# Sparse attention and a mixture of experts on one core: other lists for the experts computed early, whole-row gathers, other waits for indirect transfers

## The chip, the cores and the metric

The kernel runs on one core of a Trainium2 chip. The metric is the device time of one execution in microseconds (us). A core has a matrix engine (TensorE, PE), VectorE (DVE), ScalarE (ACT), GpSimd (POOL) and SyncE (SP); each works through its own instructions in order. In this kernel SP issues all plain transfers and POOL all indirect ones (rows gathered or scattered by a list of indices in SBUF). 16 DMA engines move the data.

## The reference

Attention with 8 batches, 8 heads, 576 positions and head size 64. Heads 0 to 3 are local (a query sees itself and the 31 positions before it), heads 4 to 7 strided (it sees earlier positions equal to its own modulo 32). The result is `x`, 4608 tokens by 512, and goes through eight experts, two for each token:

```
scores = where(mask, q @ k.T / sqrt(64), -1e9)
x      = softmax(scores) @ v                    # [4608, 512]
noisy  = x @ w_gate + log1p(exp(x @ w_noise)) * noise
top2   = the two largest of 8;  top2_w = softmax over these two
out[t] = sum over its two experts: top2_w * (relu(x[t] @ w1[e]) @ w2[e])
```

`w1[e]` is 512 x 1024 and `w2[e]` 1024 x 512, all in float32.

## The kernel before, in words

**Order.** The program is written as `Piece` objects (engine, planned duration, a function that emits instructions, a rank, dependencies). `issue_all` plays them through a planner: for each engine it takes, of the pieces that could start within 120 ns of the first, the one with the lowest rank, and emits it. So the order on every engine is fixed beforehand by planned times. The planner has a model of the DMA engines: `wire` is the time at which they are done, each transfer adds its bytes times `wires` over 270 bytes per ns, and SP's transfers aren't planned far ahead of it. `t0` is a piece's earliest time; `far` is added after a transfer that a piece depends on. A transfer marked `bulk` waits until the model is nearly idle. A piece that writes a PSUM tile and is followed by one that writes a ring buffer starts no earlier than that buffer's first writer: so the first matmul of `layer2` is planned no earlier than the transfer in `previous` that fetches the old output rows, and that one needs the zero fills of those rows.

**Attention.** 32 units (batch, pair of heads, strided or local), in turn. `loads` fetches k, q and v two units ahead, `prep` transposes k and q, `products` makes the scores of both heads, `item` the softmax and the values, `finish` stores the result to `x_dram` and transposes it into `xT`. In `x_dram` a token's 512 numbers lie as four rows of 128, 576 rows apart.

**Routing.** After the four units of a batch, `route` computes its gates and top 2, gives each (token, expert) a place in the expert's list, and writes 12 groups of 96 entries (token, weight, row) to the table `tab` by indirect transfers from POOL (L817). 

**Experts.** A list of at most 1216 places is cut into jobs of two or three blocks of 128 tokens; the last has a half block. `SUBS` names the jobs as (first place, blocks, tail, batches): a job with fewer than 8 batches takes only places that the first batches are known to fill (`AHEAD` keeps later entries behind them), and can be computed while attention is still running. There are 32 jobs and 80 whole blocks. For a job, `gather` reads the entries, makes row indices (`gxx` for x, `gix` for the output) and fetches x by four indirect transfers for each block, each 128 partitions by 512 B (L946): 32 tokens a transfer, so that DVE's transpose of 32x32 squares in `transposes` (L970) turns it into the layout that matmuls need. x is then split into a high and a low part (ACT L974, DVE L976), and so are the weights (`weights_of`, L887 and L888). `layer1` (L1002) multiplies with 96 matmuls a job, `layer2` (L1064) with 24 a block; the output rows are fetched (`previous`, L1042), added to, and scattered back (L1094). Output rows start as zeros, which SP writes in twelve fills of 384 rows (L1148).

In the planner, matmuls of the experts and of attention share PE: for each us of attention one us of expert work may go first (`PACE` 1.0).

**Pacing on POOL.** So that POOL's indirect transfers don't run ahead of the plan, each is given a wait in `issue_all` for the step of ACT or DVE that ends last at least 200 ns before it, by the plan.

Of the kernel before, what the change touches and what calls it, by code (L numbers as in the profile page):

```python
# [22 lines left out]
def kernel(  # L23
# [35 lines left out]
    AHEAD = {2: [(0, 256)], 4: [(0, 512), (1, 256)], 5: [(1, 640)], 7: [(2, 896)]}  # L59
# [99 lines left out]
    v_s = [keep.tile([GP, 2, NJ, D + 1], F32, name=f"v_s{i}") for i in range(2)]  # L159
# [25 lines left out]
    nc.gpsimd.iota(xrow, pattern=[[4 * S, B], [TB, T]], base=0, channel_multiplier=1)  # L185
    qoff = consts.tile([128, 1], F32, name="qoff")
    for i in range(4):
        nc.vector.memset(qoff[32 * i:32 * i + 32, :], float(i * S))
# [102 lines left out]
    def issue_all(expert_banks, t_start):  # L291
# [43 lines left out]
        while ready:  # L335
# [79 lines left out]
    for name, shape, dtype, depth in (  # L415
            ("raw", [LP, 2, LJ, D], F32, 2), ("ord", [LP, LJ, 2, D], F32, 1),
            ("ks", [GP, 2, NJ, D], F32, 1), ("qs", [GP, 2, NJ, D], F32, 1),
            ("mx", [128, 5], F32, 3), ("ex", [128, 5, KW], F32, 2), ("aT", [128, 5, 128], F32, 2),
            ("rs", [128, 6], F32, 2),
            ("xT", [128, S], F32, 6),  # L420
# [14 lines left out]
    def loads(u, rank):  # L435
# [21 lines left out]
        if local:  # L457
# [4 lines left out]
                             [[D, QB], [QB * D, 2 * NBL], [1, D]], 589824)], True)  # L462
# [5 lines left out]
        else:  # L468
            put("v", R["v_s"].new(),
                [(lambda t, h=h: t[:rows, h, :, :D], v, base + h * S * D, [[NJ * D, rows], [D, NJ], [1, D]], 2048 * rows)  # L470
                 for h in range(2)], True)
# [176 lines left out]
    def finish(u, xo, rank):  # L648
# [3 lines left out]
        base = (b * 4 + d) * S * 128  # L652
# [4 lines left out]
        if local:  # L657
            store(lambda t: t[:, :4, :, :].rearrange("r g h d -> r g (h d)"), 0,
                  [[128, 128], [128 * 128, 4], [1, 128]], 262144)
            store(lambda t: t[:QB, 4, :, :].rearrange("r h d -> r (h d)"), 512 * 128, [[128, QB], [1, 128]], 32768)  # L660
        else:
            for half in range(2):

# [583 lines left out]
```

## Time and profile before

| what | us |
|---|---|
| three runs | 1113.36, 1115.05, 1119.16 (median 1115.05) |
| the profiled execution | 1116.99 |
| its span, first to last instruction | 1115.2 |
| PE busy (matmul) | 1066.9 |
| DVE busy | 615.2 |
| ACT busy | 429.9 |
| POOL busy | 606.9 |
| mean granted TensorE clock | 0.970 |

Busy time is the time in which an engine has an instruction at work; matmuls are pipelined, so that of PE says little of how well it is used. Rows of instructions in order of time have the start, the duration, engine, line, operation, output and inputs, a count, and in brackets the idle time before and what ended it. Rows of groups have the line, engine and operation, the shapes, the count, total busy us and mean ns of one, and after a second bar the idle time before them.

### The profile page before, as it was taken

How to read it: one execution, taken by the hardware profiler on the slowest of the kernel's cores; microseconds unless marked ns; L12 is line 12 of the kernel's file. 1: busy time of each engine (PE TensorE's matmuls, PEld its weight loads, DVE VectorE, ACT ScalarE, POOL GpSimd, SP SyncE). 2: the span in 40 equal slices, each digit the busy share in tenths (PEclk: the TensorE clock that was granted, in tenths of full speed). 3: DMA queues.
4: the chain of work that ended last, by engine and by line, in shares of the span. 5: the costliest groups of instructions: out<-in, count | busy, mean ns of one | idle time of the engine just before them, and what ended most of it. 6: DMA issues, size and time to landing. Idle time of an engine off the chain costs nothing.

```text
span 1115.2 us, 23354 instructions
## 1 busy us (share of the span) xinstructions
PE 1066.9 (96%) x8581; PEld 940.5 (84%) x8581; DVE 615.2 (55%) x1618; ACT 429.9 (39%) x1103; POOL 606.9 (54%) x789
## 2 busy tenths in 40 slices
PE   7988889899998999999999999999999999999993
PEld 5767669788887989898998989898988898898992
DVE  4787976867764434655673455345534643473430
ACT  5687966856633211423341223123311321151220
POOL 1044464566656765656666555655646474656510
PEclk6898979999999999999999999999999999999997
DMA  9698997879775532445553226324522452253210
GB/s 189 165 204 199 229 219 172 184 199 248 198 203 102 161 88 72 135 145 148 176 165 117 83 78 195 95 61 115 174 74 68 126 164 69 77 161 92 73 42 22
DMA packets 184886, 153.03 MB, mean 137 GB/s; under 512 B 74695, under 2 KB 155079, under 8 KB 184752
## 3 DMA queue, kind: packets, MB, share of 16 engines
q1 hardware_dynamic: 159664, 92.40, 34.3%
q0 software_dynamic: 25088, 58.87, 17.7%
q8 instruction: 81, 1.33, 0.5%
q14 instruction: 53, 0.43, 0.1%
HBM read 112.86 MB, written 39.39 MB: 137 GB/s over the span
## 4 chain that ended last, share of the span: by engine, by line
PE 66%; DMA 0%; DVE 0%; issue 0%; POOL 0%; POOLq 0%; DVEq 0%
PE bankE L1064 5%; PE bankF L1064 5%; PE bankH L1064 4%; PE bankD L1064 4%; PE bankB L1064 4%; PE bankB L1002 4%; PE bankD L1002 4%; PE bankF L1002 4%; PE bankC L1002 4%; PE bankH L1002 4%; PE bankE L1002 4%; PE bankA L1002 4%; PE bankG L1002 4%; PE bankC L1064 4%; PE bankA L1064 4%; PE bankG L1064 3%
## 5 line engine op out<-in xcount | busy, mean ns | idle before, releaser
L946 POOL DMA_INDIRECT xg<-x_dram,gxx x304 | 307.4, 1011 | 145.0 <-issue 69.9
L1094 POOL DMA_INDIRECT out_dram<-prev,tabt x80 | 83.3, 1041 | 105.0 <-DVE prev L1089 38.5
L817 POOL DMA_INDIRECT tab<-ent,addr x96 | 93.4, 973 | 62.5 <-issue 10.3
L1042 POOL DMA_INDIRECT prev<-out_dram,gix x80 | 78.3, 979 | 80.5 <-DMA out_dram<-prev,tabt 29.4
L970 DVE STREAM_TRANSPOSE xr<-xg 128x512 f32<-128x512 f32 (+1 forms) x80 | 84.3, 1054 | 20.2 <-DMA xg<-x_dram,gxx 18.5
L974 ACT CAST xhi<-xr 128x512 fp32r<-128x512 f32 (+1 forms) x80 | 47.7, 596 | 95.7 <-DVE xr L970 92.7
L976 DVE TENSOR_TENSOR xlo<-xr,xhi 128x512 fp32r<-128x512 f32 (+1 forms) x80 | 53.2, 665 | 26.4 <-ACT xhi L974 25.0
L888 DVE TENSOR_TENSOR w1lo<-wraw,w1hi 128x512 fp32r<-128x512 f32 x80 | 55.0, 690 | 6.6 <-ACT w1hi L887 4.3
L887 ACT CAST w2hi<-wraw 128x512 fp32r<-128x512 f32 x80 | 46.7, 617 | 29.4 <-DMA wraw<-in_moe_w_dram 8.4
L888 DVE TENSOR_TENSOR w2lo<-wraw,w2hi 128x512 fp32r<-128x512 f32 x80 | 52.1, 682 | 3.9 <-ACT w2hi L887 3.3
L887 ACT CAST w1hi<-wraw 128x512 fp32r<-128x512 f32 x80 | 48.6, 614 | 2.5 <-DMA wraw<-in_moe_w_dram 2.4
L1002 PE MATMUL bankB<-xhi,w1hi 128*128 128x256 f32 (+3 forms) x128 | 39.4, 308 | 2.6 <-ACT xhi L974 2.6
L1002 PE MATMUL bankG<-xhi,w1hi 128*128 128x256 f32 (+3 forms) x136 | 41.1, 302 | 0.0
L1002 PE MATMUL bankG<-xhi,w1lo 128*128 128x256 f32 (+3 forms) x136 | 40.7, 300 | 0.0
L1002 PE MATMUL bankG<-xlo,w1hi 128*128 128x256 f32 (+3 forms) x136 | 40.5, 298 | 0.0
L1002 PE MATMUL bankE<-xhi,w1hi 128*128 128x256 f32 (+3 forms) x132 | 39.9, 302 | 0.0
L1002 PE MATMUL bankD<-xhi,w1hi 128*128 128x256 f32 (+3 forms) x132 | 39.8, 302 | 0.0
L1002 PE MATMUL bankC<-xhi,w1hi 128*128 128x256 f32 (+3 forms) x132 | 39.7, 301 | 0.0
L1002 PE MATMUL bankB<-xlo,w1hi 128*128 128x256 f32 (+3 forms) x128 | 38.8, 303 | 0.7 <-DVE xlo L976 0.7
L1002 PE MATMUL bankD<-xhi,w1lo 128*128 128x256 f32 (+3 forms) x132 | 39.4, 298 | 0.0
L1002 PE MATMUL bankC<-xhi,w1lo 128*128 128x256 f32 (+3 forms) x132 | 39.4, 298 | 0.0
L1002 PE MATMUL bankE<-xhi,w1lo 128*128 128x256 f32 (+3 forms) x132 | 39.4, 298 | 0.0
(614 smaller groups left out, 3474.3 us busy)
## 6 DMA issues: line engine op xcount, KB each, us to landing
wraw<-in_moe_w_dram SPq DMA_DIRECT2D x160, 256.0 KB
out_dram<-zeros SPq DMA_DIRECT2D x12, 768.0 KB
xg<-x_dram,gxx POOLq DMA_INDIRECT x304
ks<-in_k_dram SPq DMA_DIRECT2D x15, 320.0 KB
qs<-in_q_dram SPq DMA_DIRECT2D x15, 320.0 KB
v_s<-in_v_dram SPq DMA_DIRECT2D x30, 160.0 KB
raw<-in_k_dram SPq DMA_DIRECT2D x16, 288.0 KB
v_l<-in_v_dram SPq DMA_DIRECT2D x16, 288.0 KB
```

The lines of the kernel that those rows point to most:

```text
L817: st = nc.gpsimd.indirect_dma_start(out=tab, out_offset=bass.IndirectOffsetOnAxis(ap=s["addr"].t[:, t, kk:kk + 1], axis=0), in_=s["ent"].t ...
L887: Piece("ACT", act(512) + 30, lambda o: nc.scalar.copy(hi.t, raw.t), rank, read=[raw], alloc=[hi], expert=True)
L888: Piece("DVE", dve(512), lambda o: nc.vector.tensor_tensor(lo.t, raw.t, hi.t.bitcast(F32), ALU.subtract), rank, read=[raw, hi], alloc=[lo] ...
L946: dma(lambda o, i=i, g=g, xg=xg: nc.gpsimd.indirect_dma_start(out=xg.t[:, g, :], out_offset=None, in_=x_dram[:4 * known, :], in_offset=bas ...
L970: Piece("DVE", dve(4 * rows), lambda o, xg=xg, xr=xr, ng=ng, rows=rows: nc.vector.transpose(xr.t[:, :, :rows].rearrange("p c (g i) -> p g ...
L974: Piece("ACT", act(4 * rows), lambda o, xr=xr, rows=rows, cols=cols: nc.scalar.copy(xh.t[:, :, cols], xr.t[:, :, :rows]), rank, read=[xr], ...
L976: Piece("DVE", dve(4 * rows), lambda o, xr=xr, rows=rows, cols=cols: nc.vector.tensor_tensor(xl.t[:, :, cols], xr.t[:, :, :rows], xh.t[:, ...
L1002: nc.tensor.matmul(ps.t[:, :width], a.t[:, 128 * d:128 * d + 128], c.t[:, d, :width], start=(m == 0), stop=(m == len(todo) - 1))
L1042: dma(lambda o: nc.gpsimd.indirect_dma_start(out=pv.t[:rows, :], out_offset=None, in_=out[:known, :], in_offset=bass.IndirectOffsetOnAxis( ...
L1064: nc.tensor.matmul(ps.t, HT[n, f][p[0]].t[:, cols], W2[n][f][p[1]].t, start=(m == 0), stop=(m == len(todo) - 1))
L1094: st = nc.gpsimd.indirect_dma_start(out=out[:known, :], out_offset=bass.IndirectOffsetOnAxis(ap=tb.t[:rows, i, 0:1], axis=0), in_=pv.t[:ro ...
```

## The change

- **Early lists.** Jobs known early follow the lists of two, three, five and seven batches: 14 blocks in six jobs, where there were 16 blocks in seven (two, four, five and seven batches). Their `gather` has a rank by batch (`turn`), as their entry and weight loads had before.
- **Whole rows.** `x_dram` now holds a token's 512 numbers in one piece. Early jobs fetch a block with one transfer, 2 KB for each of 128 partitions, by the output's indices; they read no `tabx` and make no `gxx`. Their transposes are four matmuls on PE into a PSUM bank, reading every fourth number. Jobs over all batches gather as before, with other row numbers.
- **Stores.** Strided units store x in pieces of 512 B instead of 1 KB.
- **Strided values** are loaded in lines of 2 KB into a buffer `vraw` and copied to their places by ACT or DVE. The `xT` ring has 5 buffers instead of 6.
- **Pacing.** An indirect transfer waits for DVE's last step in its time, and for ACT's only where DVE has none.
- **Planner's figures.** v's local load counts its real bytes (half of before), narrow rows cost 1.65 instead of 1.45, local k and q 1.2 instead of 1.0, DVE's transposes 8 ns a row instead of about 4, entry loads start 4 us after the scatters; zero fills are due at 26, 36, 46, 56, 66 us and then from 111 us in steps of 10, instead of from 50 in steps of 18.

```diff
-    AHEAD = {2: [(0, 256)], 4: [(0, 512), (1, 256)], 5: [(1, 640)], 7: [(2, 896)]}
+    AHEAD = {2: [(0, 256)], 3: [(1, 384)], 5: [(1, 640), (2, 640)], 7: [(2, 896)]}
-        [(0, 2, 0, 2), (256, 2, 0, 4), (512, 3, 0, B), (896, 2, 64, B)],
-        [(0, 2, 0, 4), (256, 3, 0, 5), (640, 2, 0, B), (896, 2, 64, B)],
-        [(0, 3, 0, 7), (384, 2, 0, 7), (640, 2, 0, 7), (896, 2, 64, B)],
+        [(0, 2, 0, 2), (256, 3, 0, B), (640, 2, 0, B), (896, 2, 64, B)],
+        [(0, 3, 0, 3), (384, 2, 0, 5), (640, 2, 0, B), (896, 2, 64, B)],
+        [(0, 3, 0, 5), (384, 2, 0, 5), (640, 2, 0, 7), (896, 2, 64, B)],
...
-                behind = [x for m in marks.values() for x in m[-40:] if x[0].end + 200 <= t]
-                if behind:
-                    x = max(behind, key=lambda x: x[0].end)
-                    if x[0].end > paced[0]:
+                for engine in ("DVE", "ACT"):
+                    behind = [x for x in marks[engine][-40:] if paced[0] < x[0].end <= t - 200]
+                    if behind:
+                        x = max(behind, key=lambda x: x[0].end)
                         for y in last if isinstance(last, list) else [last]:
                             tc.add_manual_dep(...)
+                        break
...
-                    nbytes, rank, wires={D: 1.45, 4 * D: 1.2}.get(dims[-1][1], 1.0),
+                    nbytes, rank, wires={D: 1.65, LJ * D: 1.2}.get(dims[-1][1], 1.0),
...
+            slot = res["v"] = R["v_s"].new()
+            for h in range(2):
+                put(f"v{h}raw", R["vraw"].new(), [(lambda t: t[:rows].rearrange("p j d -> p (j d)"), v, base + h * S * D,
+                                                   [[NJ * D, rows], [1, NJ * D]], 2048 * rows)], True)
+                def spread(o, h=h, raw=res[f"v{h}raw"]):
+                    copy(o.e, slot.t[:G, h, :, :D], raw.t[:G])
+                Piece("ANY", {"ACT": act(NJ * D), "DVE": 75 + 0.52 * NJ * D}, spread, rank, ...)
...
-        base = (b * 4 + d) * S * 128
+        base = b * S * DM + d * 128
...
+        def turn(n):
+            hb = jobs[n][1][3]
+            return None if hb == B else 20 * NP * (hb - 1) + 10 * NP
         def gather(n, rank):
             e, (start, nb, tail, hb) = jobs[n]
+            rank = rank if hb == B else turn(n)
+            whole = hb < B
...
+            for i in range(nb) if whole else ():
+                xg = R["xg"].new()
+                dma(lambda o, i=i, xg=xg: nc.gpsimd.indirect_dma_start(
+                    out=xg.t.rearrange("p g c -> p (g c)"), out_offset=None,
+                    in_=x_dram.rearrange("(t q) c -> t (q c)", q=4)[:known, :],
+                    in_offset=bass.IndirectOffsetOnAxis(ap=gi.t[:, i:i + 1], axis=0)),
+                    262144, rank, eng="POOL", read=[gi], after=known_stores[hb], expert=True, alloc=[xg])
...
+                if hb < B:
+                    xr = Slot()
+                    def tr(o, xg=xg, xr=xr):
+                        xv = xg.t.rearrange("p g c -> p (g c)").rearrange("p (x c) -> p c x", c=ND)
+                        for c in range(ND):
+                            nc.tensor.transpose(xr.t[:, 128 * c:128 * c + 128], xv[:, c, :], ident)
+                    Piece("PE", 108 * ND, tr, rank, read=[xg], psum=xr, expert=True)
...
-            ER - 1, t0=50000 + 18000 * c, bulk=True))
+            ER - 1, t0=26000 + 10000 * c + 35000 * (c >= 5), bulk=True))
```

More of the change, by code (lines that the diff above doesn't have):

```diff
@@ L158 @@
     v_l = [keep.tile([KW, 2, NBL, D + 1], F32, name=f"v_l{i}") for i in range(2)]
-    v_s = [keep.tile([GP, 2, NJ, D + 1], F32, name=f"v_s{i}") for i in range(2)]
+    v_s = [keep.tile([G, 2, NJ, D + 1], F32, name=f"v_s{i}") for i in range(2)]
     v_0 = [keep.tile([G, 2, D + 1], F32, name=f"v_0{i}") for i in range(2)]
@@ L468, in loads @@
         else:
-            put("v", R["v_s"].new(),
-                [(lambda t, h=h: t[:rows, h, :, :D], v, base + h * S * D, [[NJ * D, rows], [D, NJ], [1, D]], 2048 * rows)
-                 for h in range(2)], True)
+            slot = res["v"] = R["v_s"].new()
[4 more added lines that the diff above has]
+                    copy(o.e, slot.t[:G, h, :, :D], raw.t[:G])
+                Piece("ANY", {"ACT": act(NJ * D), "DVE": 75 + 0.52 * NJ * D}, spread, rank, read=[res[f"v{h}raw"]],
+                      **{"write" if h else "alloc": [slot]})
             put("v0", R["v_0"].new(),
@@ L664, in finish @@
                 store(lambda t, half=half: t[64 * half:64 * half + 64, :4, :, :].rearrange(
-                    "r (m g) h d -> r m (g h d)", m=2),
-                      (QB + 2 * half) * 128, [[NJ * 128, QB], [4 * 128, 2], [1, 256]], 131072)
-            store(lambda t: t[:QB, 4, :, :].rearrange("r h d -> r (h d)"), 0, [[128, QB], [1, 128]], 32768)
+                    "r (m g) h d -> r m g (h d)", m=2),
+                      (QB + 2 * half) * DM, [[NJ * DM, QB], [4 * DM, 2], [DM, 2], [1, 128]], 131072)
+            store(lambda t: t[:QB, 4, :, :].rearrange("r h d -> r (h d)"), 0, [[DM, QB], [1, 128]], 32768)
         xt = R["xT"].new()
@@ L863 @@
             ("tabt", [128, 3, 3], I32, 3), ("gix", [128, 3], I32, 3), ("tabx", [128, 12, 3], I32, 2),
-            ("gxx", [128, 3, 4], I32, 2), ("xg", [128, 4, 128], F32, 2), ("xr", [128, ND, 128], F32, 1),
+            ("gxx", [128, 3, 4], I32, 2), ("xg", [128, 4, 128], F32, 2), ("xr", [128, ND * 128], F32, 1),
             ("xhi", [128, ND, WID], F32R, 1), ("xlo", [128, ND, WID], F32R, 1),
@@ L899, in experts @@
         G_, XH, HT = {}, {}, {}
+        def turn(n):
+            hb = jobs[n][1][3]
+            return None if hb == B else 20 * NP * (hb - 1) + 10 * NP
         def gather(n, rank):
             e, (start, nb, tail, hb) = jobs[n]
+            rank = rank if hb == B else turn(n)
             known = hb * S
-            tb, gi, tx, gx = R["tabt"].new(), R["gix"].new(), R["tabx"].new(), R["gxx"].new()
+            whole = hb < B
+            tb, gi = R["tabt"].new(), R["gix"].new()
+            tx, gx = (None, None) if whole else (R["tabx"].new(), R["gxx"].new())
             def entries(dst, p0, n, how, bytes_, dims):
@@ L916, in load @@
                         early_loads.append((ld, hb))
-                dma(load, bytes_, rank if hb == B else 20 * NP * (hb - 1) + 10 * NP, after=known_tab[hb], expert=True, **how)
-            entries(lambda: tx.t[:, :4 * nb, :].rearrange("p b c -> p (b c)"), start, 128 * nb, {"alloc": [tx]}, 16384,
-                    [[0, 4], [12 * nb, 32], [1, 12 * nb]])
+                dma(load, bytes_, rank if hb == B else 20 * NP * (hb - 1) + 10 * NP, after=known_tab[hb], expert=True,
+                    far=4000, **how)
+            if not whole:
+                entries(lambda: tx.t[:, :4 * nb, :].rearrange("p b c -> p (b c)"), start, 128 * nb, {"alloc": [tx]}, 16384,
+                        [[0, 4], [12 * nb, 32], [1, 12 * nb]])
             ng = tail // 32
@@ L931, in gather @@
                         [[3, tail], [1, 3]])
-            rows_known = 4 * known - 3 * S - 1
+            rows_known = 4 * known - 4
             def xindices(o):
@@ L939, in xindices @@
                                             qoff[:, 0:1], op0=ALU.min, op1=ALU.add)
-            Piece("POOL", 360 if tail else 230, xindices, rank, read=[tx] + ([tx2] if tail else []), alloc=[gx],
-                  expert=True)
+            if not whole:
+                Piece("POOL", 360 if tail else 230, xindices, rank, read=[tx] + ([tx2] if tail else []), alloc=[gx],
+                      expert=True)
             xs = []
-            for i in range(nb + (tail > 0)):
+            for i in () if whole else range(nb + (tail > 0)):
                 xg = R["xg"].new()
@@ L965, in transposes @@
             for i in range(nb + (tail > 0)):
-                xg, xr = G_[n][2][i], R["xr"].new()
+                xg = G_[n][2][i]
                 rows = 128 if i < nb else tail
@@ L1101, in layer2 @@
             out_done[e].append(dma(scatter, rows * 2048, rank, eng="POOL", read=[pv, tb], expert=True))
-        def turn(n):
-            hb = jobs[n][1][3]
-            return None if hb == B else 20 * NP * (hb - 1) + 10 * NP
         W2 = {}
```

35 lines of the change are left out of this document (20 added, 15 removed).

## The prediction

> **What bounds the kernel now.** I read the page's head first, then the busy time by stretch, then PE's waits and the POOL and SP queues in order of time where PE is not full.
>
> ```profile
> span 1115.2 us, 23354 instructions
> ...
> PE 1066.9 (96%) x8581; PEld 940.5 (84%) x8581; DVE 615.2 (55%) x1618; ACT 429.9 (39%) x1103; POOL 606.9 (54%) x789
> ```
>
> The next rows cut the span into stretches. Columns: window, its length, then busy us of PE, PEld, DVE, ACT, POOL, the granted TensorE clock, the DMA share, GB/s.
>
> ```profile
> 0.00:132.00 132.00, 112.81 (x1719) 91.65 (x1719) 96.57 (x411) 98.57 (x297) 36.97 (x98) 0.87 0.90 194
> 132.00:160.00 28.00, 24.43 (x369) 19.72 (x369) 22.61 (x101) 20.77 (x64) 18.35 (x31) 0.84 1.10 234
> 160.00:220.00 60.00, 55.30 (x848) 47.45 (x845) 45.11 (x165) 43.21 (x138) 32.34 (x57) 0.93 0.86 185
> 220.00:340.00 120.00, 119.47 (x1305) 103.88 (x1304) 85.00 (x309) 67.69 (x190) 74.45 (x115) 1.00 0.80 207
> 340.00:380.00 40.00, 36.75 (x177) 32.88 (x176) 18.29 (x28) 11.05 (x22) 26.42 (x34) 0.96 0.52 135
> 380.00:1100.00 720.00, 718.10 (x4176) 644.94 (x4174) 347.61 (x607) 188.61 (x397) 418.26 (x458) 1.00 0.37 110
> 1100.00:1115.00 15.00, 0.00 (x0) 0.00 (x0) 0.00 (x0) 0.00 (x0) 0.15 (x1) 0.61 0.05 20
> ```
>
> From 380 to 1100 PE idles 1.9 us in 720 at full clock. That part is matmul work which the change leaves alone: 80 blocks and 32 jobs before and after, with the same widths. The last 15 us are the final scatter and the end. So the time can change only before 380 us, by PE's idle time, its clock, or its work. There, attention alone does not fill PE; expert blocks computed early do. While they run (220 to 340) PE is full, before that it is not.
>
> Where the early work starts is read from the queues. First POOL:
>
> ```profile
> 112.20 0.91 POOL L817 DMA_INDIRECT tab<-ent,addr  x1 [0.21 <-DVE mx L576]
> ...
> 144.12 1.06 POOL L946 DMA_INDIRECT xg<-x_dram,gxx  x1 [1.23 <-issue]
> ...
> 154.24 0.94 POOL L946 DMA_INDIRECT xg<-x_dram,gxx  x1 [1.10 <-DVE ns L791]
> ```
>
> Then SP's issues, then PE:
>
> ```profile
> 119.07 0.66 SPq L908 DMA_DIRECT2D tabx<-tab  x1
> ```
>
> ```profile
> 175.10 0.63 SPq L1148 DMA_DIRECT2D out_dram<-zeros  x1
> ```
>
> ```profile
> 167.78 0.36 PE L1002 MATMUL bankB<-xhi,w1hi 128*128 128x256 f32 x1
> ```
>
> ```profile
> 220.19 0.48 PE L1064 MATMUL bankD<-w2hi,hhi 128*128 128x512 f32 x1
> ```
>
> The table entries of batches 0 and 1 are written by 113.1 and read at 119, but the first gather starts at 144, behind batch 2's twelve table scatters on POOL, and takes eight transfers to 155. Layer 1 of the first job starts at 168. Its layer 2 starts only at 220, since the planner puts it no earlier than the fetch of the old output rows, which needs three of the zero fills; the second is issued at 175, the third after it.
>
> **The change, part by part.**
>
> *Early jobs first in their turn, one gather a block, zero fills earlier.* A job with a list known early now has its gather ranked by batch, so ahead of batch 2's scatters; it needs no tabx load and no gxx step, and 2 transfers where there were 8. A gather lands like this in the chain that ended last:
>
> ```profile
> 355.67 3.52 DMA xg<-x_dram,gxx
> ```
>
> From the entry load at 119 I estimate 3.5 us to land (taken as for a gather), 2.5 for two transfers of 1.27, 3.5 to land, and 1.9 for transposes and both splits (0.46 and twice 0.69, rows below). That is 130.4 at the earliest; I take 138, for the 4 us that the planner now adds after the scatters and for the queues' order. With fills due from 26 us in steps of 10, layer 2 follows layer 1, and a three-block list of batch 2 comes next instead of a two-block list of batch 3.
>
> What PE then wins, by window, as idle plus clock loss (busy x (1 - clock)):
> - 132 to 160: 3.57 + 24.43 x 0.16 = 7.5; with work from 138 on I count 5.0.
> - 160 to 220: 4.70 + 55.30 x 0.07 = 8.6; I count 8.0, as 220 to 340 shows 0.5 idle in 120 us with early work at hand.
> - 340 to 380: 3.25 + 36.75 x 0.04 = 4.7. This is a gather behind the last scatters:
>
> ```profile
> 347.63 0.91 POOL L817 DMA_INDIRECT tab<-ent,addr  x1 [0.23 <-issue]
> 348.85 0.97 POOL L946 DMA_INDIRECT xg<-x_dram,gxx  x1 [0.30 <-issue]
> ...
> 355.67 1.27 POOL L946 DMA_INDIRECT xg<-x_dram,gxx  x1 [0.85 <-ACT xhi L974]
> ```
>
> The third block of a three-block early job is fetched after batch 7's scatters. The new list for seven batches is two blocks, fetched by two transfers that go ahead of those scatters. I count 4.5.
>
> Together -17.5 us, between 0 and -20.8.
>
> *Transposes of the 14 early blocks move from DVE to PE.* Four 128x128 transposes a block:
>
> ```profile
> 111.66 0.63 PE L681 MATMUL bankH<-ident,xo 128*128 128x128 f32 x4 [1.04 <-DVE xo L630]
> 112.12 0.60 PE L590 MATMUL bankB<-ident,ex 128*72 128x128 f32 x4
> ```
>
> Four such cost 0.46 us of PE's time to the next instruction, so 14 x 0.46 = +6.4 us, all of it on the path, as PE is full by then. Up to 0.63 each, 8.8, without overlap. DVE loses 14 transposes:
>
> ```profile
> L970 DVE STREAM_TRANSPOSE xr<-xg 128x512 f32<-128x512 f32 x72 | 79.3, 1101 | 20.0 <-DMA xg<-x_dram,gxx 18.5 <-issue 0.4
> L976 DVE TENSOR_TENSOR xlo<-xr,xhi 128x512 fp32r<-128x512 f32 x72 | 49.7, 691 | 22.6 <-ACT xhi L974 21.3
> ...
> L283 ACT COPY ord<-raw 96x768 f32<-96x768 f32 x26 | 21.6, 832 | 0.8 <-PE bankC L497 0.3
> ```
>
> 14 x 1.10 = 15.4 us of DVE while PE is the bound: 0.
>
> *Values of the strided heads in long lines, then spread.* Each of 32 loads has 80 packets of 2 KB instead of 640 of 256 B (two of them 72 and 576), and a copy of 72x512 is added. By the 768-wide ACT copy that is at most 0.55 us, 32 in all. Only what lies before the early work counts: in 132 us some 3.3 of 8 batches, 13 copies, 7.2 us of engine time. DVE and ACT are 73 and 75% busy there, and PE waits there for them:
>
> ```profile
> PE bankA L681 <- DVE xo L630: 2.0, 1, 2.0
> PE bankF L609 <- ACT aT L283: 1.4, 1, 1.4
> PE bankA L497 <- ACT ord L283: 1.1, 1, 1.1
> ```
>
> So between 0 and +7.2; as two engines share it and a quarter of them is free, I take +1.5. The packets:
>
> ```profile
> q1 hardware_dynamic: 159664, 92.40, 34.3%
> ```
>
> 34.3% of 16 x 1115.2 us over 159,664 packets is 38 ns a packet. 30 x 560 + 2 x 504 = 17,808 packets fewer are at most 42.6 us of all 16 engines, 17 of it before 132, and nothing if time goes by bytes. The x_dram stores of the strided heads now go in 512 B pieces instead of 1 KB: 32 x 128 packets more, at most 9.8 us by the same price. Five zero fills of 786 KB brought before 132 cost 4.1 us each at 194 GB/s: 20 us at most. DMA is 90% busy there, but what ends PE's waits is DVE and ACT, and loads are issued two units ahead; I take 0 for the net, between -3 and +8, the planner's halved bytes for v_l and its other new prices included, since they only change when SP issues; if that cover is gone a fill holds the loads behind it on SP's queue by its 4.1 us.
>
> *POOL.* 42 transfers fewer:
>
> ```profile
> L946 POOL DMA_INDIRECT xg<-x_dram,gxx x304 | 307.4, 1011 | 145.0 <-issue 69.9 <-DVE xr L970 22.4 <-ACT hhi L1021 17.3
> ```
>
> 42 x 1.01 = 42 us off POOL, which is 54% busy: 0 by itself. Putting each transfer behind a DVE step rather than the latest of DVE and ACT can only choose an earlier or equal step while a DVE step lies in the window, so it costs nothing as long as DVE keeps to its plan; what is queued behind such a wait are the table scatters and gathers, and PE would wait for them. Bounds: all 17.3 us of waits on ACT gone or as many new ones on DVE, off PE's path but for the first gather; 0. The xT ring of 5 instead of 6 still holds a batch's four and one more: 0. SP issues fewer tabx loads; the entry loads' 4 us exist in the plan only.
>
> *Handover to the whole lists.* 14 early blocks instead of 16 have to last until the first gather over all batches. Block cost, layer 1 of a three-block job (8 groups) and layer 2:
>
> ```profile
> 378.46 2.08 PE bankA L1002 x12
> 380.54 5.58 PE bankB L1064 x24
> ```
>
> 8 x 2.08 / 3 + 5.6 = 11.15 us a block, so 156 + 6.4 = 162.5 us. Batch 7's gate is here:
>
> ```profile
> 318.49 1.50 PE L727 MATMUL bankB<-xT,wg 128*32 128x192 f32 x24
> ```
>
> Its scatters end at 348.5, 30 us later; then some 22.2 us by the durations above (entries 3.5, ten transfers at 1.27, landing 3.5, DVE transpose and splits 2.5): 52.2 in all. The expert matmuls of 132 to 318 are two groups:
>
> ```profile
> 132.00:318.00 186.00, 39.99 (x288) 35.54 (x288) 0.95 0.87 205
> ```
>
> ```profile
> 132.00:318.00 186.00, 33.44 (x125) 22.09 (x126) 0.95 0.87 205
> ```
>
> By the stretches above PE works about 177 us in that time, so attention is 104 of it. The kernel gives early work at most an equal share, so 104 are used by the gate and 58.5 are left for 52.2. Before, 178 - 73 = 105 were left. The cover just holds; I take +0.5, between 0 and +18 (if the route is as slow as that or the share is passed).
>
> **Sum.** -17.5 + 6.4 + 1.5 + 0.5 = -9.1. The profiled execution took 1116.99 (its span and 1.8 around it): 1107.9. It stands 1.9 above the median of the three runs, so I predict 1106 for the median. 0.5% is 5.6 us, about what a measurement of this kernel can tell from no change.
>
> **The rivals.**
>
> *The early stage gains too (0.13).* Against me: 19.2 us idle and a clock of 0.87 before 132, with DMA at 90%. If the long lines let loads land sooner, a third of the first stretch's idle goes, about 6 to 9 us more: 1098. What speaks against it: the waits end on DVE and ACT, which get more work.
>
> *Transposes with a 16-byte step cost PE double (0.14).* The new transposes read every fourth word of a row. DVE's transpose reads so too and takes 1101 ns, where its subtraction of as many elements takes 691; no matmul of this trace loads its weights with such a step. Doubled, the four cost 0.92 us: +6.4 more, and 1112.5, no change. A rule speaks for it: the Trainium skill, page "SBUF — State Buffer", section "Door 1: The DMA port swizzle", says that SBUF is read in lines of 16 bytes, and that accesses which go to a new line each time pay for it. It gives no price; the two DVE rows agree in direction.
>
> *The gap is filled late (0.12).* The second early job is now another expert's, so 16 weight tiles must be loaded and split between 140 and 175, where the DMA share is 0.86 or more and DVE and ACT are 72 to 81% busy. If its layer 1 waits until about 200, half of the 13.0 goes: 1112.5, no change.
>
> *Starved at the handover (0.16).* Place: between the end of the 14 blocks and the first gather over eight batches. Price: one us of idle per us of cover missing, the clock falling with it. It decides the sign when 15 us are missing, that is when the route from gate to splits takes 73 us instead of 52.2, or early work passes its share by that much: 1124. For it: two blocks, 22 us, fewer. Against it: attention alone never ran as slowly as that.
>
> **How the numbers follow.** My forecast has 0.45 (1106, by itself 1101 to 1110); 0.13 for 1098, 0.14 and 0.12 for 1112.5, 0.16 for 1124. Faster is 0.45 + 0.13 = 0.58, same 0.26, slower 0.16. The range is 1094 to 1120: the low end is all of the 20.8 and some of the early stage, the high end leaves out most of the last case.
>
> **What would show it.** Right: the first L1002 matmul by 140 and the first L1064 soon after; 132 to 220 with under 2 us idle and the clock at 1.00; 14 groups of four transposes at about 0.46 us; no idle between 340 and 400; 262 rather than 304 gathers. Wrong: groups of four transposes near 0.9 us; PE waiting for xhi after the last early block; a first stretch longer because loads queue behind zero fills.

## The result and the profile after

The changed kernel takes 1108.62 us (median; 1103.93 to 1112.45 over 6 runs), the kernel before 1115.88 us beside it (1113.36 to 1119.16, 6 runs): a ratio of 0.9927, 95% interval 0.9901 to 0.9952. In a later session, beside other kernels, it took 1107.69 against 1116.11, ratio 0.9928 (0.9903 to 0.9953). So it is 0.7% faster, 2.6 us from the predicted 1106. The medians differ by 7.3 us. The two profiled executions, 1116.99 and 1107.29, differ by 9.7, since the one is slower and the other faster than its median. How these 9.7 us came about is another matter.

The head of the page, two of its groups and its main DMA queue:

```profile
span 1105.5 us, 23346 instructions
...
PE 1064.2 (96%) x8637; PEld 939.5 (85%) x8637; DVE 605.6 (55%) x1604; ACT 434.7 (39%) x1135; POOL 563.3 (51%) x741
...
q1 hardware_dynamic: 145160, 92.31, 33.4%
...
L964 POOL DMA_INDIRECT xg<-x_dram,gxx x248 | 255.1, 1029 | 101.8 <-issue 55.2
...
L978 POOL DMA_INDIRECT xg<-x_dram,gix x14 | 14.3, 1024 | 57.1 <-PE bankB L1003 40.4
```

There are 248 + 14 = 262 gathers, as forecast, and one number that was not: of the 57.1 us that POOL idled ahead of whole-row gathers, 40.4 were one kind of wait, on PE.

The stretches, with the columns of those shown of before (PE, PEld, DVE, ACT, POOL, clock, DMA share, GB/s):

```profile
0.00:132.00 132.00, 115.26 (x1780) 93.40 (x1782) 103.01 (x422) 100.44 (x314) 38.68 (x96) 0.90 0.93 210
132.00:160.00 28.00, 27.29 (x388) 23.59 (x385) 23.72 (x102) 24.68 (x73) 13.26 (x24) 1.00 0.89 211
160.00:220.00 60.00, 54.09 (x885) 45.96 (x887) 48.40 (x177) 48.49 (x151) 29.24 (x56) 0.94 0.96 222
220.00:340.00 120.00, 119.48 (x1228) 104.26 (x1221) 70.86 (x271) 61.59 (x178) 39.57 (x68) 1.00 0.61 165
340.00:380.00 40.00, 35.65 (x206) 31.52 (x205) 15.97 (x29) 10.69 (x23) 25.69 (x44) 1.00 0.56 159
380.00:1090.00 710.00, 710.00 (x4166) 639.13 (x4165) 342.87 (x606) 188.85 (x398) 415.86 (x455) 1.00 0.37 112
```

PE's loss in a stretch, reckoned as in the prediction (idle time plus busy time by one minus the clock):

| stretch | before | after | gained | predicted |
|---|---|---|---|---|
| 0 to 132 | 33.9 | 28.3 | 5.6 | -1.5 (the copies) |
| 132 to 160 | 7.5 | 0.7 | 6.8 | 5.0 |
| 160 to 220 | 8.6 | 9.2 | -0.6 | 8.0 |
| 220 to 340 | 0.5 | 0.5 | 0 | 0 |
| 340 to 380 | 4.7 | 4.35 | 0.4 | 4.5 |

That is 12.2 us in all. Busy time by the clock, summed over the stretches, is PE's work: 1042.9 us before and 1049.4 after (with its last 2.4 us, behind 1090, at full clock), 6.5 more, which I read as the new transposes. The 6.5 is not exact: the clock is given with two digits, and 0.005 of it is 0.6 us in the first stretch and 3.6 in the last. And the ends differ: POOL's last scatter in each kernel, before and then after.

```profile
1099.17 0.98 POOL L1094 DMA_INDIRECT out_dram<-prev,tabt  x1 [4.12 <-DVE prev L1089]
```

```profile
1093.50 0.98 POOL L1134 DMA_INDIRECT out_dram<-prev,tabt  x1 [4.09 <-DVE prev L1129]
```

From there to the end of the span it is 16.0 us before (1115.2 - 1099.17) and 12.0 after (1105.5 - 1093.50), with nothing busy but the transfer itself, whose packets are through some 2.5 us after its issue in both. Together 12.2 - 6.5 + 4.0 = 9.7, the whole difference. This sum has to come out, as what a stretch does not lose is counted as work; it checks the arithmetic and not the causes. So two of the three gains that I forecast did not come, and two came that I had not counted (the first stretch and the end).

Where the first two early jobs stand (PE, SP and POOL in order of time):

```profile
146.47 0.38 PE L1042 MATMUL bankB<-xhi,w1hi 128*128 128x256 f32 x1
...
215.96 0.50 PE L1104 MATMUL bankB<-w2hi,hhi 128*128 128x512 f32 x1
```

```profile
69.06 0.60 SPq L1184 DMA_DIRECT2D out_dram<-zeros  x1
...
203.51 1.44 SPq L1184 DMA_DIRECT2D out_dram<-zeros  x1
```

```profile
213.07 0.98 POOL L1082 DMA_INDIRECT prev<-out_dram,gix  x1 [0.55 <-DVE aT L286]
```

Layer 1 starts 21 us sooner (146.5 for 167.8). Layer 2 does not follow: 216.0 for 220.2. Its first matmul is planned behind the fetch of the old rows at 213, that behind the third zero fill, and the third fill is issued at 203.5, though it was due at 46. A fill is a bulk transfer, and those wait until the model of the DMA engines is nearly idle; after the second, at 69, that is not so for 134 us.

The other stretch, on POOL and then on DVE:

```profile
276.61 0.94 POOL L824 DMA_INDIRECT tab<-ent,addr  x1 [0.22 <-POOL spacer L823]
...
317.94 0.98 POOL L978 DMA_INDIRECT xg<-x_dram,gix  x1 [40.39 <-PE bankB L1003]
...
339.46 0.99 POOL L1082 DMA_INDIRECT prev<-out_dram,gix  x1 [3.29 <-issue]
```

```profile
344.63 0.75 DVE L1129 SCALAR_TENSOR_TENSOR prev<-bankA,tabt,prev 128x512 f32<-128x512 f32 x1 [18.44 <-DMA prev<-out_dram,gix]
```

The gather at 317.94 is the third block of a three-block job. There are two `xg` buffers, so it can't start before PE has transposed that job's first block, and POOL stands for 40 us after the first of a batch's twelve table scatters. The rest of these scatters, the fetch of old rows at 339 and DVE's sum at 344.6 come late in turn, and PE idles 4.35 us between 340 and 380.

### The profile page after: what moved, and what is told of

Read it like the earlier page. It is cut to its first block, busy times and chain, and to the rows that moved or that the text cites. A ratio compares the mean times of both kernels' runs of the same rounds, so it can differ in the third digit from the quotient of the medians.

```text
span 1105.5 us, 23346 instructions
## 1 busy us (share of the span) xinstructions
PE 1064.2 (96%) x8637; PEld 939.5 (85%) x8637; DVE 605.6 (55%) x1604; ACT 434.7 (39%) x1135; POOL 563.3 (51%) x741
## 3 DMA queue, kind: packets, MB, share of 16 engines
q1 hardware_dynamic: 145160, 92.31, 33.4%
## 4 chain that ended last, share of the span: by engine, by line
PE 83%; DMA 6%; ACT 4%; DVE 3%; issue 1%; POOL 1%; SPq 0%; POOLq 0%; DVEq 0%; ACTq 0%
PE bankB L1104 6%; PE bankG L1104 5%; PE bankE L1104 5%; PE bankA L1104 5%; PE bankE L1042 5%; PE bankC L1042 5%; PE bankC L1104 5%; PE bankF L1042 5%; PE bankD L1042 5%; PE bankA L1042 4%; PE bankB L1042 4%; PE bankF L1104 4%; PE bankH L1042 4%; PE bankG L1042 4%; PE bankH L1104 4%; PE bankD L1104 3%
## 5 line engine op out<-in xcount | busy, mean ns | idle before, releaser
L964 POOL DMA_INDIRECT xg<-x_dram,gxx x248 | 255.1, 1029 | 101.8 <-issue 55.2
L824 POOL DMA_INDIRECT tab<-ent,addr x96 | 92.7, 965 | 57.1 <-issue 20.4
L1007 DVE STREAM_TRANSPOSE xr<-xg 128x512 f32<-128x512 f32 (+1 forms) x66 | 68.5, 1039 | 23.5 <-DMA xg<-x_dram,gxx 21.1
L1014 ACT CAST xhi<-xr 128x512 fp32r<-128x512 f32 (+1 forms) x66 | 39.0, 591 | 72.9 <-DVE xr L1007 72.9
L1016 DVE TENSOR_TENSOR xlo<-xr,xhi 128x512 fp32r<-128x512 f32 (+1 forms) x66 | 43.5, 659 | 19.2 <-ACT xhi L1014 17.9
L978 POOL DMA_INDIRECT xg<-x_dram,gix x14 | 14.3, 1024 | 57.1 <-PE bankB L1003 40.4
L1042 PE MATMUL bankH<-xhi,w1hi 128*128 128x256 f32 (+3 forms) x128 | 38.6, 302 | 1.4 <-DVE prev L1129 1.4
L1042 PE MATMUL bankA<-xhi,w1hi 128*128 128x256 f32 (+3 forms) x128 | 38.3, 299 | 1.7 <-DVE prev L1129 1.7
L1042 PE MATMUL bankE<-xlo,w1hi 128*128 128x256 f32 (+3 forms) x132 | 39.2, 297 | 0.0
L1042 PE MATMUL bankF<-xhi,w1hi 128*128 128x256 f32 (+3 forms) x128 | 38.3, 300 | 0.0
```

The source lines that it names most:

```text
L824: st = nc.gpsimd.indirect_dma_start(out=tab, out_offset=bass.IndirectOffsetOnAxis(ap=s["addr"].t[:, t, kk:kk + 1], axis=0), in_=s["ent"].t ...
L964: dma(lambda o, i=i, g=g, xg=xg: nc.gpsimd.indirect_dma_start(out=xg.t[:, g, :], out_offset=None, in_=x_dram[:4 * known, :], in_offset=bas ...
L978: dma(lambda o, i=i, xg=xg: nc.gpsimd.indirect_dma_start(out=xg.t.rearrange("p g c -> p (g c)"), out_offset=None, in_=x_dram.rearrange("(t ...
L1007: Piece("DVE", 8 * rows, lambda o, xg=xg, xr=xr, ng=ng, rows=rows: nc.vector.transpose(xr.t.rearrange("p (c x) -> p c x", c=ND)[:, :, :row ...
L1014: Piece("ACT", act(4 * rows), lambda o, view=view, cols=cols: nc.scalar.copy(xh.t[:, :, cols], view()), rank, read=[xr], expert=True, **{h ...
L1016: Piece("DVE", dve(4 * rows), lambda o, view=view, cols=cols: nc.vector.tensor_tensor(xl.t[:, :, cols], view(), xh.t[:, :, cols].bitcast(F ...
```

## The experiments

The kernels ran in three groups of four, each group on one chip and beside the kernel before. On the second of these chips the kernel before took 1116.11 us; on the first and third 1171.88 and 1171.06. Ratios of different chips are not set against each other below.

**First chip (before: 1171.88, 1167.87 to 1181.37).** First, three zero fills ahead of the bulk rule:

```diff
-            ER - 1, t0=26000 + 10000 * c + 35000 * (c >= 5), bulk=True))
+            35 + 20 * c if c < 3 else ER - 1, t0=26000 + 10000 * c + 35000 * (c >= 5), bulk=c >= 3))
```

> The first three zero fills are issued ahead of other transfers (due at 26, 36, 46 us) instead of when the transfer model is idle; all else as in the changed kernel. My theory: the hole that stays in PE from 170 to 216 us (5.9 us idle in 160 to 220 and a clock of 0.94, 9.1 us lost together) is there because layer 2 of the first early job is planned behind the fetch of old output rows, and that behind the third fill, issued at 203. Then layer 2 starts by about 175, 160 to 220 loses under 3 us, and the kernel takes 1099 to 1104. Rival: the hole is the second early job's weights, or the transfers' load, and early fills only push loads back: layer 2 still late or a longer first stretch, 1107 to 1113.

Measured: 1151.08, ratio 0.982 (0.9787 to 0.9853). Layer 2 comes at 180.8, near the 175 of the theory, but 160 to 220 loses 8.5 us and not under 3. Next, the third gather behind the batch's scatters:

```diff
-                    262144, rank, eng="POOL", read=[gi], after=known_stores[hb], expert=True, alloc=[xg])
+                    262144, rank if i < 2 else ER, eng="POOL", read=[gi], after=known_stores[hb], expert=True, alloc=[xg])
```

> The third block of a three-block early job is gathered at the low rank of the expert work, so behind the table scatters of the batch; all else as in the changed kernel. My theory: with two xg buffers the third gather waits on POOL until PE has transposed the first block (40.4 us at 277 to 318), which holds the scatters of batch 6, then a fetch of output rows, on which DVE waits 18.4 us and PE 4.4 us in 340 to 360. Then no POOL wait above 20 us, PE idle in 340 to 380 under 1.5 us, and 1103 to 1107. Rival: that wait is covered and the idle time at 340 comes from the weights that land late (wraw waits of 20 us on ScalarE): no change, 1107 to 1110.

Measured: 1141.58, ratio 0.9755 (0.9718 to 0.9791). Neither sign of the theory came: POOL still waits 23.1 us, and PE idles 4.8 us from 340 to 380. Then the strided values as before:

```diff
-            slot = res["v"] = R["v_s"].new()
-            for h in range(2):
-                put(f"v{h}raw", R["vraw"].new(), ...)
...
+            put("v", R["v_s"].new(),
+                [(lambda t, h=h: t[:rows, h, :, :D], v, base + h * S * D, [[NJ * D, rows], [D, NJ], [1, D]], 2048 * rows)
+                 for h in range(2)], True)
```

> The changed kernel with the strided values loaded in short lines of 256 B straight to their places, as before, without vraw and the spreading copies. My theory: the first 132 us got 5.7 us cheaper (idle 19.2 to 16.7, clock 0.87 to 0.90) because the long lines relieve the DMA engines; undone, the first stretch loses 3 to 6 us again: 1111 to 1115. Rival: that part is the planner's new order, and the copies on ScalarE and VectorE cost what the packets save: 1106 to 1110.

Measured: 1160.86, ratio 0.9893 (0.985 to 0.9936). Its first 132 us lose 34.7, where the others of this chip lose 34.6 to 36.6; the third chip takes this up again. Last, the old pacing:

```diff
-                for engine in ("DVE", "ACT"):
-                    behind = [x for x in marks[engine][-40:] if paced[0] < x[0].end <= t - 200]
...
+                    behind = [x for m in marks.values() for x in m[-40:] if x[0].end + 200 <= t]
```

> The changed kernel with the old rule for POOL's waits: the latest step of ScalarE and VectorE rather than VectorE's. My theory: POOL is off the path except for the first gathers, so nothing within the measurement: 1106 to 1111. Rival: the waits on ScalarE held the scatters and gathers, and this is a good part of the gain: 1112 to 1116.

Measured: 1156.94, ratio 0.9877 (0.9834 to 0.992).

What follows. The changed kernel itself did not run on this chip, so the four can only be set against each other. Among them the late third gather is the fastest, by 9.5 us and more. The stretches 220 to 340 of the early fills and then of the late third gather:

```profile
220.00:340.00 120.00, 106.00 (x1228) 87.64 (x1227) 63.85 (x233) 62.97 (x185) 40.86 (x69) 0.91 0.71 188
```

```profile
220.00:340.00 120.00, 114.31 (x1342) 95.92 (x1339) 72.04 (x263) 68.58 (x206) 44.01 (x80) 1.00 0.71 190
```

With fills alone, layer 2 starts sooner (180.8, where the late gather has 236.5). The early work is used up while POOL stands 33.1 us before a third gather (from 320 to 340 PE runs no layer 1 and idles 8.2 us): the idle time has only moved. The wait is still there, 39.99 us long, with the old pacing, which clears the new pacing of it. With the third gather late, POOL also waits for PE before it, 23.1 us, but after the last table scatter of that batch (at 320.84); the next batch's begin at 367.

**Second chip (before: 1116.11, 1112.7 to 1120.0, 11 runs).** The changed kernel itself:

> The changed kernel itself, unchanged, as the partner of the other runs. Theory (what the first trace of it showed is planned into the kernel, not an accident of that run): layer 1 of the first early job between 140 and 160 us, its layer 2 not before 200 us because the third zero fill is issued after 195 us, and one wait of 30 to 45 us on GpSimd ahead of a third whole-row gather. Ratio to the kernel before 0.980 to 0.993. Rival (the first trace caught one unlucky execution): third fill and third gather without those waits here, and a ratio near 0.980.

Measured: 1107.69 (1104.46 to 1110.94). Third fill at 201.6, layer 1 at 144.2, layer 2 at 214.0, one wait of 40.39 us on POOL. The theory holds: what the first trace showed is in the order of the program.

Both repairs together (the two edits above):

> Two edits together: the first three zero fills get an early rank of their own, and the third gather of a three-block early job gets the experts' rank (behind the batch's table scatters). Theory (two separate waits, both of the plan): the first layer 2 comes by 200 us instead of after 200 to 234, no wait of over 20 us on GpSimd ahead of a third gather; PE's idle time and clock loss from 160 to 380 us fall below that of either edit alone; 0.970 of the kernel before or less, 5 us or more under the late third gather alone. Rival (early work that starts sooner is also used up sooner, and the fills hold loads behind them in the first stretch): the gap moves to between 300 and 420 us, and the time is equal to or up to 8 us above that of the late third gather alone (0.9755).

Measured: 1106.58, ratio 0.9913 (0.9888 to 0.9938). The rival is right about the place (between 300 and 420 us); its time can't be set against the late gather's alone, which ran on another chip. The stretches:

```profile
0.00:132.00 132.00, 113.94 (x1721) 92.52 (x1725) 101.06 (x424) 96.48 (x303) 37.12 (x95) 0.86 0.96 211
...
160.00:220.00 60.00, 59.41 (x731) 52.27 (x730) 45.88 (x154) 44.28 (x125) 30.88 (x52) 1.00 0.90 223
...
340.00:380.00 40.00, 40.00 (x254) 34.22 (x253) 13.53 (x54) 6.83 (x19) 17.40 (x32) 1.00 0.14 42
380.00:420.00 40.00, 30.68 (x176) 27.25 (x175) 10.71 (x20) 5.66 (x13) 18.81 (x22) 0.88 0.22 64
```

```profile
170.28 0.48 PE L1104 MATMUL bankD<-w2hi,hhi 128*128 128x512 f32 x1
```

Layer 2 starts at 170 and both predicted gains appear in full: 160 to 220 loses 0.6 us, 340 to 380 none. They are given back twice. The first stretch loses 34.0 us for the changed kernel's 27.1 beside it, with the three fills issued at 30, 42 and 56; and at the handover the early work has run out, 9.3 us idle and 3.7 us of clock between 380 and 420.

The early gathers at the experts' rank again, which puts a third gather behind the scatters too:

```diff
-            rank = rank if hb == B else turn(n)
```

> One part undone: the early jobs' gathers have the experts' rank again instead of one by their batch; the lists, transposes, whole-row gathers, fills and long lines stay. Theory (the new rank is what brings the first early job forward, and also what puts a third gather ahead of the scatters): the first whole-row gather moves from 130 to 140 us or later and layer 1 of the first job to 158 us or later, 2 to 5 us lost before 220 us; the 30 to 45 us wait on GpSimd is gone, 3 to 5 us won between 300 and 400 us; time within 4 us of the changed kernel. Rival (the rank is the gain and the wait costs nothing, as GpSimd is half idle): 5 us or more slower than the changed kernel.

Measured: 1104.32 (1102.39 to 1105.21), ratio 0.9892 (0.9868 to 0.9915), 3.4 us under the changed kernel.

```profile
132.00:160.00 28.00, 25.89 (x416) 21.43 (x412) 25.80 (x108) 24.55 (x80) 15.51 (x29) 1.00 1.08 240
160.00:220.00 60.00, 55.36 (x850) 47.46 (x852) 47.15 (x170) 47.89 (x144) 27.58 (x50) 0.97 0.90 210
...
340.00:380.00 40.00, 40.00 (x240) 36.38 (x239) 10.42 (x19) 7.36 (x17) 19.84 (x26) 1.00 0.31 91
```

```profile
274.85 0.96 POOL L977 DMA_INDIRECT xg<-x_dram,gix  x1 [2.87 <-PE bankB L1002]
...
317.88 0.98 POOL L977 DMA_INDIRECT xg<-x_dram,gix  x1 [7.80 <-PE bankB L1002]
```

The theory holds, with a smaller cost than it gave: the first gather moves to 142.8 and layer 1 to 156.8, 132 to 160 loses 2.1 us where the changed kernel beside it loses 0.4, and up to 220 it loses 37.6 us for 37.0. No gather waits longer than 7.8 us, and PE is full from 340 to 380. The new rank of the early gathers is worth less than the wait that it makes. This is the fastest version measured on this chip. The intervals of the two ratios overlap (0.9903 to 0.9915), but both hold the spread of the kernel before; set directly against each other, the six runs of each put it 1.4 to 6.1 us under the changed kernel (an estimate of 95% from their spread).

The old early lists:

```diff
-    AHEAD = {2: [(0, 256)], 3: [(1, 384)], 5: [(1, 640), (2, 640)], 7: [(2, 896)]}
+    AHEAD = {2: [(0, 256)], 4: [(0, 512), (1, 256)], 5: [(1, 640)], 7: [(2, 896)]}
...
```

> One part undone: the early lists are again those for two, four, five and seven batches with sixteen early blocks; everything else is new. Theory (the gain before 160 us comes from rank and single gathers, not from which lists exist): layer 1 of the first job still between 140 and 160 us; two more early blocks cost 8 more transposes, 1.1 us; time from 2 us faster to 4 us slower than the changed kernel. Rival (the lists carry the gain): back to within 5 us of the kernel before, with PE idle time of 5 us or more coming back between 160 and 340 us.

Measured: 1106.62 (1103.55 to 1110.17), 1.1 us under the changed kernel; the six runs of each can't show a difference of less than about 3 us. Layer 1 comes at 145.5. The theory holds: the new lists are not what made the kernel faster. With sixteen blocks the loss moves (160 to 220 loses 5.4 us, 220 to 340 7.7), and layer 2 starts at 180.4, as the third fill finds an idle moment at 153.5.

**Third chip (before: 1171.06, 1166.33 to 1179.21).** The third fill alone brought forward, on the kernel with the experts' rank:

```diff
-            ER - 1, t0=26000 + 10000 * c + 35000 * (c >= 5), bulk=True))
+            95 if c == 2 else ER - 1, t0=26000 + 10000 * c + 35000 * (c >= 5) + 64000 * (c == 2), bulk=c != 2))
```

> The kernel with the experts' rank for the early gathers, and only the third zero fill brought forward, to about 110 us, ahead of the bulk rule; the first two fills stay where they are. Theory (layer 2 of the first early job waits for the fetch of the old rows, that for the third fill; and the first stretch lost 6 us when all three fills went ahead of its loads): first layer 2 before 185 us instead of after 215, idle time plus clock loss of 160 to 220 us under 3 us instead of 6.2, the first stretch within 1.5 us of the same kernel without the edit; 4 us or more off, if no new gap opens at the handover: 0.983 to 0.987 of the kernel before. Rival (early work that starts sooner is used up sooner): the same gain at 160 to 220 us, and as much idle time between 340 and 420 us; 0.988 to 0.991, no change against the experts' rank alone.

Measured: 1164.44 (1155.7 to 1167.87), ratio 0.9911 (0.9874 to 0.9948). The same with `PACE = 0.85`:

> As the run before it, and PACE from 1.0 to 0.85: early work gets at most 0.85 us for each us of attention. Theory (the handover is the second bound: what early work is left when attention ends is the cover for the route to the first gather over all batches): idle time between 340 and 420 us under 1 us, with the gain at 160 to 220 us kept; 0.981 to 0.986 of the kernel before. Rival (the handover was covered already, and the smaller share only thins the work in the early stretches): idle time of 132 to 340 us rises by 2 us or more and the time is equal to or above that of the run before it.

Measured: 1154.73 (1149.64 to 1155.57), ratio 0.983 (0.9791 to 0.9869). On this chip the first job's layer 1 comes only at 178 in both, layer 2 at 203.3 and 201.6, so neither shows what the fill brings where layer 1 comes at 145, and both miss their theory (160 to 220 loses 11.3 and 8.7 us). The smaller share is 9.7 us faster, with intervals that do not meet, but not in the place I named: 340 to 380 idles more (15.5 us for 6.2), 220 to 340 less (7.0 for 12.4). The largest difference lies behind the window that I named: from 420 to 1000 PE loses 3.0 us (all idle) instead of 15.8 (10.1 idle). That would fit a handover that is better covered and comes later than I took it, but no run tests it. That the share matters is shown; how is not.

The short loads of strided values once more:

> One part undone: the strided heads' values are again loaded in 256-byte pieces straight to their places, with no copies behind; the rest is new. On the first chip it was tried on, where the kernel before took 1172 us, its first stretch could not be set beside one of the changed kernel. Theory (the long lines are what shortened the first 132 us): idle time plus clock loss of 0 to 132 us back at 32 to 35 us, against 27 to 29 in the new kernel and 33.9 in the kernel before; 4 us or more slower than the changed kernel (ratio 0.997 or more). Rival (the first stretch is shorter by the planner's new prices and by GpSimd's new pacing, and the copies cost what the long lines bring): 27 to 30 us in that stretch, and a time within 3 us of the changed kernel's (0.990 to 0.995).

Measured: 1158.29, ratio 0.9886 (0.9844 to 0.9927). Its first stretch loses 35.7 us. The runs with long lines on this chip lose 31.3 (the one below), 32.7 and 35.3 there, so over 132 us nothing can be told. Divided at 30 us, the traces do tell. The first transposes of a local unit's k on PE, in the kernel before and the changed one, then with short lines and with long ones on this chip:

```profile
17.66 0.74 PE L497 MATMUL bankH<-ident,ord 96*128 96x96 f32 x3
```

```profile
9.98 0.47 PE L505 MATMUL bankG<-ident,ord 96*128 96x96 f32 x3
```

```profile
17.76 0.69 PE L499 MATMUL bankH<-ident,ord 96*128 96x96 f32 x3
```

```profile
9.96 0.47 PE L505 MATMUL bankG<-ident,ord 96*128 96x96 f32 x3
```

| traces | SP issues that k | its transposes | PE loses in 15 to 30 | in 30 to 132 |
|---|---|---|---|---|
| before | 7.4 | 17.7 | 8.6 | 19.2 |
| changed kernel | 3.7 | 10.0 | 2.2 | 21.8 |
| the three with short lines (before; first and third chip) | 7.4 to 7.7 | 17.4 to 17.8 | 7.4 to 8.7 | 19.2 to 22.7 |
| the eleven with long lines, all chips | 3.7 | 10.0 to 10.2 | 1.9 to 3.5 | 18.5 to 28.6 |

So the edit to long lines does shorten the start, by 4.6 to 6.6 us in 15 to 30 on the first and third chip, and the planner's new prices and the new pacing, which the two kernels with short lines keep, do not. What it changes there is the order: a head's values go through `vraw`, which has one buffer, so the second head's load waits for the copy and the local unit's k goes ahead of it. Whether cheaper packets help too is not separated. On the first and third chip the gain is spent again between 30 and 132.

The DMA queue shows what the packets cost. The page of the short lines, then of the long ones (packets, MB, share of the 16 engines), whose spans are 1150.6 and 1148.4:

```profile
q1 hardware_dynamic: 162968, 92.31, 32.5%
```

```profile
q1 hardware_dynamic: 145160, 92.31, 32.1%
```

Last, the price of the 16-byte step:

```diff
-                        xv = xg.t.rearrange("p g c -> p (g c)").rearrange("p (x c) -> p c x", c=ND)
+                        xv = xg.t.rearrange("p g c -> p (g c)").rearrange("p (c x) -> p c x", c=ND)
```

> The PE transposes of the early blocks read 128 consecutive numbers of a row instead of every fourth: the early blocks' channels come in another order, so this run shows only the price of the step. Theory (the 16-byte step is what makes these weight loads slower than those of the attention transposes): their weight loads fall from 213 ns to 137 to 145 ns, and four transposes from 0.55 to about 0.46 us. Rival (it is the source tile or the time at which they run): 200 ns or more still.

Measured, in one run: the weight loads of one bank's transposes, in the changed kernel and then here (minimum, median, maximum in ns; first and last start):

```profile
L1003 PEld LDWEIGHTS bankB<-ident,xg x12: 196/213/221, 267.7 to 353.7; 128*128 128x128 f32 x12
```

```profile
L1003 PEld LDWEIGHTS bankB<-ident,xg x12: 138/140/142, 294.0 to 388.0; 128*128 128x128 f32 x12
```

The same group of four, changed kernel first, each with the next instruction on PE:

```profile
172.66 0.72 PE L1003 MATMUL bankA<-ident,xg 128*128 128x128 f32 x4 [0.66 <-DMA xg<-x_dram,gix]
173.22 0.41 PE L505 MATMUL bankB<-ident,ord 96*128 96x96 f32 x3
```

```profile
187.43 0.60 PE L1003 MATMUL bankA<-ident,xg 128*128 128x128 f32 x4
187.87 0.41 PE L505 MATMUL bankB<-ident,ord 96*128 96x96 f32 x3
```

The step makes a weight load 1.5 times as long, and four transposes 0.56 instead of 0.44 us.

## Why the prediction was right in its time and only partly in its reasons

**132 to 160.** Right in size, 6.8 us for 5.0, and in part for the reason given: the first transposes are there by 138, layer 1 at 146.5 and not by 140. With the early gathers back behind the scatters the first transposes come at 149.9 and layer 1 at 156.8, and the stretch still loses only 2.1 of the 7.5. So the gathers' rank is worth 1.7. Single gathers are the next cause that I named, and from first gather to layer 1 it is 14 us there where it was 24; but before 150, with no early work on PE in either, PE idles 0.9 us there and 3.1 in the kernel before, and that share has another cause, which stays open.

**160 to 220.** Wrong. The step that failed is "with fills due from 26 us in steps of 10, layer 2 follows layer 1". I took a due time for an issue time. I had quoted the third fill's part in holding up layer 2, and did not ask what lets a bulk transfer go. The early fills together with the late third gather won the stretch back in full (0.6 us lost), so the mechanism is shown; they also show that the 8.0 would not have stood in the sum, since 13.0 us came back at the handover.

**340 to 380.** Wrong. The step is "two transfers that go ahead of those scatters". That is true of the new last list, but an earlier list has three blocks, and the rank that puts gathers ahead of scatters puts its third one there too, with two buffers to gather into. A wait that used to lie behind the scatters was moved in front of them. I named no such rival. The experts' rank for the gathers undid it, and the stretch was full.

**0 to 132.** Wrong. The forecast was a loss of 1.5, and I gave 0.13 to the rival that the early stage gains. It gained 5.6, near that rival's 6 to 9. Four traces of new kernels without early fills lose 27.1 to 29.2 there where before takes 1116, against 33.9 in the one trace of before. The step that failed is "what ends PE's waits is DVE and ACT, and loads are issued two units ahead; I take 0 for the net". A step of ACT can itself hang on a load: with the first local k issued at 3.7 us instead of 7.4, ACT's first copy `ord<-raw` starts at 8.0 instead of 14.5, and 15 to 30 alone loses 2.2 for 8.6. The short lines undo this on two chips. That early fills would cost nothing there was hardly put to the test, as only two went before 132 (at 49 and 69) where one did before. With three of them issued by 56 us the stretch loses 34.0 for 27.1 to 29.2 of the other new kernels on that chip, inside my bound of 8; on the first chip the kernel with early fills loses only 1.4 to 2.0 more than the two others with long lines.

**Packets.** I bounded 17,808 fewer packets by 42.6 us of all engines, and by nothing if time goes by bytes. The two rows above give (32.5% x 1150.6 - 32.1% x 1148.4), 5.3 us of all 16 engines. But the kernels with long lines differ as much among themselves: on this chip the other two stand at 360.0 and 364.4 us, where the row above has 368.6 and the short lines 373.9; on the first chip it is 357.9 to 361.8 for 366.3. So the saving is 4.5 to 13.9 us, a third of my bound at most. Over the loads' 20,352 short packets of 256 B each, that is 3.6 to 10.9 ns more than for the same bytes in long lines. At the queue's mean rate (92.31 MB in 5898 us of one engine) 256 B take 16.4 ns, so the short form costs between a fifth and two thirds more. The Trainium skill, page "DMA: Bandwidth & Descriptors", section "Why small descriptors are slow (HBM only)", gives a fixed overhead per packet and works it out as 27% for 256 bytes (3 of 11 cycles). Such an overhead is within what was measured here, which is too wide to confirm its size.

**Transposes.** Mis-sized by a little: 14 groups at 0.56 are 7.8 us, where I took 0.46 and 6.4 and bounded at 8.8; the difference in PE's work was 6.5. The rival of the 16-byte step was right in its mechanism and had the wrong price: not double but a quarter more of PE's time. The rule named there (accesses that go to a new 16-byte line pay) agrees with 213 against 140 ns, and the price is now measured.

**Handover.** Right for the kernel as changed: no idle time from 380 to 420. My rival of a starved handover is what the kernel meets as soon as the other gaps are closed.

**The end.** Not in the prediction at all: 4.0 of the 9.7 us lie after the last scatter is issued. All new kernels' traces have 11.2 to 12.2 us there; of the kernel before there is one trace, with 16.0. Whether that is its rule or one execution stays open; 2.4 of the 9.7 us are in any case the two executions' distance from their medians.

So the sum was right by luck, because errors cancelled. Two gains stayed out, 8.6 and 4.1 us; against these 12.7 stand 7.1 in the first stretch (5.6 and the 1.5 that I had set against it), 1.8 more at 132, 4.0 at the end and 0.5 at the handover: 13.4. With 0.1 more for PE's work, -9.1 becomes the -9.7 of the profiled executions; between the medians it was -7.3.

## What to carry to other kernels

When a load is split or routed through a buffer, look at which other load it lets go first: here a new order of the first few transfers came with 6 us less loss in the first 30 us. A due time in a plan is not a start: before counting on an earlier transfer, find the rule that releases it and the first moment at which that rule lets it go. When a rank moves a job forward, follow every instruction of it, the last ones too, and count the buffers that they need: one gather without a buffer stops all that is queued behind it. And where work is brought forward to fill a gap, look at the place where it will be missing: closing both gaps with early fills and a late third gather opened one of 13 us at the handover.

## What the runs showed of the hardware

A transpose on PE that reads every fourth float32 of a row loads its weights in 213 ns instead of 140 (128x128, medians of the two runs above).

The kernel before takes 1116 us on one chip and 1171 to 1172 us on two others, 5% more; each chip had one session. From 420 to 1090 us, matmul work of the experts, they are nearly alike (PE busy 666.7 us at a clock of 0.99 with the straight transposes on the third chip, 669.6 at 1.00 for the changed kernel on the second), and most of the time is lost while attention runs: the gate of batch 2 is at 113.9 us and that of batch 7 at 340.0 there, against 109.8 and 312.0. Between 60 and 120 us the main queue's packets took no longer there (46.8 ns of an engine each, against 48.0). The cause was not found.
